# Attention and MLP layer on one core: order of the weights of the output product, of the MLP's first pair, of V's first lower halves and of the last product's additions

## The chip, the cores and the metric

The kernel runs on one core of a Trainium2 chip. A core has TensorE (PE in the profile; its weight loads are PEld), VectorE (DVE), ScalarE (ACT), GpSimd (POOL) and SyncE (SP), whose queue issues most of the DMAs; ScalarE issues some too. Each engine works through its own instructions in order and waits on semaphores for the others. TensorE writes into PSUM, eight banks of 128 x 512 f32; the other engines read it there. The metric is device time in microseconds, the median of several runs.

## The reference

One layer on x of 2048 tokens by 1024 features, in f32:

```
h  = x + attention(layernorm(x))       # 32 heads of 32, 4 segments of 512 tokens:
                                       # softmax inside the segment + a memory (M, z) carried over
                                       # segments, mixed by sigmoid(beta); then @ wo
h2 = h + gelu(layernorm(h) @ w1 + b1) @ w2 + b2      # w1 1024 x 3584, w2 3584 x 1024
```

## The kernel before

**Numbers in two halves.** Every matmul operand is kept as an upper half, rounded to fp32r by a cast, and a lower half, the rest, made by a subtraction. A product is three matmuls (upper x upper, upper x lower, lower x upper; `mm3`, `product`); such a group of three over 128 x 512 is the smallest step below. The cast is ScalarE's or VectorE's, the subtraction VectorE's or GpSimd's (`split`, lines 91 to 96).

**Stages.** A loop goes over two halves of 1024 tokens. In each: attention for 8 groups of 4 heads and two segments; the output product for the first segment (`wo_first`), woven into the last heads; the output product for the second segment (`wo_second`), woven into the first segment's second layer norm; the MLP's first product. After both halves comes the MLP's second product for all tokens (`Second`). Both MLP products save multiplications by forming sums of blocks and seven products instead of eight (Strassen-Winograd). So operands are sums of weight blocks or of token blocks, made by GpSimd or VectorE before they are split.

**What sets the order.** In attention and in `wo_second` a scheduler of the framework orders each engine's instructions at compile time, by their place in the program and by when it estimates their data to be ready; TensorE's order in `wo_second` is pinned to the program's (`in_order`, line 99). From the MLP's first product on, every engine's order is the program's. Python generators weave two streams: `interleave(main, side, ratio)` advances the side stream by `ratio` steps per step of the main one.

**Start of the second half.** `weights(0)` (line 630) loads the first group's blocks of wk, wq and wv (512 KB each, two raw buffers, tag wr), casts the uppers and has GpSimd make each lower half in one piece (line 96). `dense` multiplies them by the first segment's normalised tokens: keys (kps), queries (qps), values (vps), eight groups each. Woven in at 1.1 side steps per group is `ln1(half, 1)`, the second segment's layer norm: for each of four tiles of 128 tokens bn_stats on VectorE, mean and variance to scale and offset in three small GpSimd operations (`ln_scale`, `ln_offset`, lines 133 to 139), an activation (line 168), then two times four transposes on TensorE, a cast (149) and a subtraction (151). The keys of the second segment follow and need all four tiles.

**`wo_second`** computes eight blocks (n, t), n the half of the output columns and t the tile of tokens, in the order (0,0) (0,1) (1,0) (1,1) (0,2) (1,2) (0,3) (1,3), eight groups each. The weights come as four pieces k per n, 512 KB each, through the same two raw buffers. The pieces of n = 1 are called for in groups 1 and 5 of the blocks (0,0) and (0,1). A hook loads the MLP's first raw weights (`begin`, line 901) into the same buffers, a later one casts and subtracts them (909, 915).

**MLP, first product.** `lead` (line 927) goes through 14 steps. A step loads w1's block j + 3, casts block j + 2, does four groups of its upper part (c1) and subtracts its lower half (915), then four groups of c2 and the gelu (882), whose result goes to DRAM from ScalarE's queue. The last two steps have no c1. Woven in at 0.4 steps per group is `ln2_last`: the second segment's layer norm, transposed, and its combinations T1 to T4 (lines 814 to 838), some eleven VectorE operations for each of four tiles. When it is done, `fetch(0)` loads the raw blocks of the first of 14 pairs and a partial product saved before (p1). A table `todo` hangs three things on steps:

```
todo = {11: lambda: mixer.combine(0), 12: lambda: mixer.fetch(1),
        13: lambda: (mixer.made(0, "S2", "S1", "S3", "A22", "S4"), mixer.combine(1))}
```

`combine` makes four sums on GpSimd (980 to 983), `made` splits five blocks (cast 995, subtraction 996). Each `pair(j)` then has four-group products on PSUM banks bps and dps; u (1010) and u3 (1022) copy the bps bank out while the product goes on accumulating in it, so the next product of that bank waits for them.

**MLP, second product.** `Second` runs 112 jobs of 21 matmuls: two passes over the hidden features, each with seven products of eight token pairs. The products "1" and "7" of a pair, and "6" and "5", share a bank: the later one adds into it after the earlier one's result has been added to the output. In the loop (line 1261) come, for job n, `product(n)` on TensorE, then `work(n)`: loads, `sums` (GpSimd, 1165 to 1174), `prep(n + 2)`, which casts and subtracts the left operand of the job after next (1188, 1189), `fill_up(n)`, which makes right operands from w2 rows (GpSimd 1117, cast 1119, subtraction 1120), further loads; then `add(n)`, which adds the job's bank to output tiles c on VectorE (1257). The tiles c are loaded from DRAM up to two jobs ahead (1202). During the last pair, `prep(0)` and `prep(1)` are done after its groups 8 and 11.

Of the kernel before, what the change touches and what calls it, by code (L numbers as in the profile page):

```python
# [42 lines left out]
def build(tc, x, wq, wk, wv, wo, beta, w1, b1, w2, b2, out):  # L43
# [300 lines left out]
    def attention(half, first):  # L344
# [285 lines left out]
        def weights(g):  # L630
            ws = {}
            for n, w in (("k", wk), ("q", wq), ("v", wv)):
                ws[n] = load_block(wp, w, g * P, 3, "vector" if g or n == "k" else "scalar")
            return ws

        ws = first or weights(0)
        prev = None
        for g in range(NG):
            for sl in range(2):
                u = {"g": g, "s": 2 * half + sl}  # L640
                d = dense(g, sl, ws, u)
                if prev is None:
                    interleave(d, ln1(half, 1, aside=ws.pop("rest", None)), 1.6 if first else 1.1)
                    if first:
                        constants()
                    if "last" in acts:
                        acts.pop("last")
                else:
                    if g == NG - 1 and sl == 1:
                        d = hooked(d, lambda k: load_o(half, 0, k, ab), 3, NG - 1)  # L650
                    interleave(d, heads(prev), 1.0)
                prev = u
            if g + 1 < NG:
                ws = weights(g + 1)
# [29 lines left out]

    def wo_raw(n, k):
        wr = wp.tile([P, DC, P], F32, tag="wr", name="wr", bufs=2).rearrange("p a b -> p (a b)").rearrange("p (c n) -> p c n", c=2)
        nc.sync.dma_start(wr, wo[k * 256:(k + 1) * 256, n * 512:(n + 1) * 512].rearrange("(c p) n -> p c n", p=P))
# [58 lines left out]

    def wo_second(half, hts, ready):

# [283 lines left out]
    class Second:  # L1032
# [243 lines left out]
    for half in range(2):  # L1276
# [35 lines left out]

        second = wo_second(half, hts1, ready)
        load_x(half, 1, hts1)
# [6 lines left out]
        def ln2_last():  # L1321
# [3 lines left out]
            for n, _ in enumerate(side):  # L1325
# [6 lines left out]
        side, acc = ln2_last(), 0.0  # L1332
        todo = {11: lambda: mixer.combine(0), 12: lambda: mixer.fetch(1),
                13: lambda: (mixer.made(0, "S2", "S1", "S3", "A22", "S4"), mixer.combine(1))}
        for _ in mixer.lead():
            acc += 0.4
            while side and acc >= 1.0:
                acc -= 1.0
                if next(side, 0) == 0:
                    side = None  # L1340
                    pp.release()
                    mp = mixer.mp = tc.alloc_tile_pool(name=f"m1{half}", bufs=1, side="right", reuse_waits="tile")
                    mixer.fetch(0)
            if mixer.step in todo and not side:
# [12 lines left out]
        else:  # L1357
# [3 lines left out]
            for j in range(HP):  # L1361
# [3 lines left out]
                for n, _ in enumerate(mixer.pair(j)):  # L1365
# [44 lines left out]
```

## Time and profile before

| | us |
|---|---|
| median of 3 runs | 2328.36 |
| lowest and highest | 2328.06, 2329.9 |
| the profiled execution's own time | 2327.21 |
| its span, first to last instruction | 2325.4 |
| TensorE busy in the span | 2279.2 |

The profile is of one execution; its times are from the span's start. Stages in it: attention of the first half to about 550, `wo_second` to about 620, MLP lead to 703, pairs to 900; the second half's to 1435, 1505, 1588 and 1782; then the last product. A row of a timeline has start, duration, engine, line, operation, output <- inputs, shapes, and in brackets the engine's idle time before it and what ended that. A row of a table of waits has who waited for whom, the total, the times and the longest. "Granted clock" is the share of full speed at which TensorE was clocked.

### The profile page before, as it was taken

Reading aid. Unit: us, or ns where it says so; the run is one execution under the profiler, and the core shown is the slowest. Engines: PE = TensorE matmul, PEld = TensorE weight load, DVE = VectorE, ACT = ScalarE, POOL = GpSimd, SP = SyncE. Lnnn points to the kernel's source line nnn. Section 1 sums busy time; section 2 is a strip of 40 time slices with the busy share of each in tenths; the row PEclk is TensorE's granted clock in tenths of the full one; section 3 lists DMA queues with packets and bytes.
Section 4 is the critical chain, followed back from the end, with each engine's and each line's share of the span. In section 5 each row is a group of like instructions: output and inputs, shape, how many; then the busy total and the mean of one; then the engine's idle time right before and its main releaser. Section 6 shows DMA issues by size and latency. Waiting matters only on the chain.

```text
span 2325.4 us, 35324 instructions
## 1 busy us (share of the span) xinstructions
PE 2279.2 (98%) x11769; PEld 1891.8 (81%) x11769; DVE 1566.8 (67%) x3295; ACT 1232.5 (53%) x2561; POOL 1021.0 (44%) x1053
## 2 busy tenths in 40 slices
PE   8999999999999999999999999999999999999999
PEld 6888888878778887888888877778887888888887
DVE  7777777776655565777777777564566776567653
ACT  6777777775453445777777776363343223323321
POOL 5444555554104442555555556203444554156440
PEclk9999999999999999999999999999999999999999
DMA  6333333345365655333333344466667976577762
GB/s 192 87 85 88 91 91 84 83 131 184 116 207 168 187 162 146 105 90 85 84 90 85 84 110 149 141 199 176 172 182 265 332 253 201 167 245 238 245 220 93
DMA packets 322721, 355.36 MB, mean 153 GB/s; under 512 B 26191, under 2 KB 218731, under 8 KB 322539
## 3 DMA queue, kind: packets, MB, share of 16 engines
q1 hardware_dynamic: 259370, 316.40, 45.2%
q10 hardware_dynamic: 63168, 36.71, 5.3%
q8 instruction: 93, 1.52, 0.3%
q14 instruction: 90, 0.73, 0.1%
HBM read 226.59 MB, written 76.09 MB: 130 GB/s over the span
## 4 chain that ended last, share of the span: by engine, by line
PE 75%; DVE 9%; ACT 7%; issue 3%; DMA 3%; POOL 2%; SPq 0%; ACTq 0%; POOLq 0%; DVEq 0%
PE po L1247 22%; PE bps L865 8%; PE dps L865 5%; PE ppt L564 5%; PE po L584 5%; PE cps L865 3%; PE vps L120 2%; PE vps L119 2%; PE vps L121 2%; PE pqk L532 2%; PE kps L119 2%; PE kps L121 2%; PE kps L120 2%; ACT pr L541 2%; DVE ptl L571 2%
## 5 line engine op out<-in xcount | busy, mean ns | idle before, releaser
L548 POOL TENSOR_SCALAR pr<-pr,nm,gate 128x128 f32<-128x128 f32 (+3 forms) x512 | 320.2, 635 | 360.5 <-DVE nm L545 272.2
L541 ACT ACTIVATE pr<-pr,mx 128x256 f32<-128x256 f32 (+3 forms) x512 | 287.7, 562 | 164.4 <-DVE mx L533 161.4
L571 DVE TENSOR_TENSOR ptl<-ppt,pth 128x512 fp32r<-128x512 f32 (+1 forms) x384 | 228.0, 600 | 81.8 <-ACT pth L566 77.3
L533 DVE CUSTOM_DVE_ANT_0 pr<-pqk,mask 128x256 f32<-128x256 f32 (+3 forms) x512 | 243.6, 484 | 39.7 <-PE pqk L532 37.9
L564 PE MATMUL ppt<-ident,pr 128*128 128x128 f32 x1280 | 222.7, 277 | 1.5 <-DVE ptl L571 1.1
L566 ACT CAST pth<-ppt 128x512 fp32r<-128x512 f32 (+1 forms) x384 | 193.6, 516 | 37.3 <-PE ppt L564 30.7
L1257 DVE TENSOR_TENSOR c<-c,po 128x512 f32<-128x512 f32 x160 | 105.3, 683 | 150.6 <-PE po L1247 150.6
L564 PEld LDWEIGHTS ppt<-ident,pr 128*128 128x128 f32 x1280 | 164.0, 140 | 32.2 <-DVE ptl L571 2.1
L96 POOL TENSOR_TENSOR wl<-wr,wh 128x1024 fp32r<-128x1024 f32 x53 | 126.8, 2392 | 85.9 <-DVE wh L93 33.6
L532 PE MATMUL pqk<-ks,qs 96*128 96x256 f32 (+3 forms) x512 | 161.4, 316 | 0.2 <-DVE mx L533 0.2
L584 PE MATMUL po<-ptl,vs 128*64 128x512 f32 (+3 forms) x512 | 154.1, 311 | 5.1 <-DVE ptl L571 4.4
L584 PE MATMUL po<-pth,vs 128*64 128x512 f32 (+3 forms) x512 | 155.9, 327 | 1.2 <-ACT pth L566 1.1
L980 POOL TENSOR_TENSOR s<-r 128x512 f32<-128x512 f32 x28 | 42.9, 1532 | 233.0 <-DVE sa L996 77.2
L1247 PE MATMUL po<-w2h,zh 128*128 128x512 f32 x378 | 120.7, 389 | 0.0
L1117 POOL TENSOR_TENSOR w2r<-w2r 128x512 f32<-128x512 f32 x54 | 87.5, 1633 | 61.7 <-DMA w2r<-in_B_w 53.9
L532 PEld LDWEIGHTS pqk<-ks,qs 96*128 96x128 f32 x512 | 96.2, 188 | 21.6 <-DVE mx L533 0.7
L865 PE MATMUL bps<-zh,sa 128*128 128x512 f32 x336 | 110.8, 391 | 1.9 <-DVE u L1010 1.9
L865 PE MATMUL bps<-zh,sb 128*128 128x512 f32 x336 | 111.0, 391 | 0.9 <-DVE u L1022 0.9
L119 PE MATMUL vps<-yh,wh 128*128 128x512 f32 x256 | 109.4, 427 | 1.1 <-DVE MZ L499 1.1
L119 PE MATMUL kps<-yh,wh 128*128 128x512 f32 (+1 forms) x264 | 110.0, 417 | 0.0
L119 PE MATMUL qps<-yh,wh 128*128 128x512 f32 x256 | 107.1, 418 | 0.0
L1247 PE MATMUL po<-w2h,hl 128*128 128x512 f32 x322 | 102.9, 389 | 1.5 <-DVE c L1257 1.5
(239 smaller groups left out, 6626.5 us busy)
## 6 DMA issues: line engine op xcount, KB each, us to landing
hr<-h_dram SPq DMA_DIRECT2D x112, 448.0 KB, 4.8
w2r<-in_B_w SPq DMA_DIRECT2D x122, 256.0 KB, 4.4
r<-in_B_w SPq DMA_DIRECT2D x56, 512.0 KB, 4.6
h_dram<-ht ACTq DMA_DIRECT2D x84, 256.0 KB, 3.8
ks<-kh SPq DMA_DIRECT2D x256, 64.0 KB, 2.0
qs<-qh SPq DMA_DIRECT2D x256, 64.0 KB, 2.0
wr<-in_A_wo SPq DMA_DIRECT2D x32, 512.0 KB, 4.0
wx<-in_B_w SPq DMA_DIRECT2D x56, 256.0 KB, 4.0
```

Source lines behind the costliest of these rows:

```text
L96: getattr(nc, lo_eng).tensor_tensor(lo, w, raw(hi), op=ALU.subtract)
L119: nc.tensor.matmul(ps, ah, bh, start=first, stop=False)
L532: nc.tensor.matmul(pqk[:, :n], u["qs"][j][:, i * P:(i + 1) * P], u["ks"][j][:, 0:n], start=True, stop=True)
L533: nc.vector.tensor_tensor_reduce(out=st["pr"][:, offs[i]:offs[i] + n], in0=pqk[:, :n], in1=mask[:, 512 - n:512], op0=ALU.add, op1=ALU.min, ...
L541: nc.scalar.activation(pi, pi, AF.Exp, bias=mx[:, i:i + 1], scale=-1.0, accum_out=mx[:, 4 + i:5 + i])
L548: nc.gpsimd.tensor_scalar(pi, pi, nm[:, 4 + k:5 + k], gate[:, 1, 4 * g + j:4 * g + j + 1], op0=ALU.mult, op1=ALU.mult)
L564: nc.tensor.transpose(ppt[:, o:o + P], pr[:, offs[i] + jk * P:offs[i] + (jk + 1) * P], ident)
L566: nc.scalar.copy(pth[:, base:base + w], ppt[:, :w])
L571: nc.vector.tensor_tensor(o, x0, x1, op=ALU.subtract)
L584: nc.tensor.matmul(po[:, P * jk:], v, st[part][:, koff[jk]:koff[jk] + w], start=(jk, part) == (0, "pth"), stop=(jk, part) == (2, "ptl"))
L865: nc.tensor.matmul(ps, x_[:, c, :], y_[:, c, :], start=first and c == 0 and n == 0, stop=last and c == 3 and n == 2, skip_group_check=True)
L1247: nc.tensor.matmul(ps, x_[:, k], y_[k], start=opens and k == 0 and i == 0, stop=closes and k == self.KP - 1 and i == 2, skip_group_check=True)
```

## The change

1. Start of the second half: the value block's lower half is no longer made in `weights(0)`. It is made in two pieces of four chunks on GpSimd, hung behind the scale and offset of the layer norm's tiles 1 and 2 (`rest`). `ln1` there yields eight times between its loads and its first statistics, and goes at 1.5 side steps per group, not 1.1. (The first half's start, with its own `first`, is as before.)
2. `wo_second`: all four pieces of n = 1 are called for in block (0,0), in groups 1, 3, 5 and 7; pieces 0 and 1 land in two raw buffers of the pool `post`, pieces 2 and 3 in the old ones.
3. MLP lead: `ln2_last` goes at 0.3 steps per group; `fetch(0)` and `combine(0)` come in step 9, `made(0)` and `fetch(1)` in step 12, `combine(1)` in step 13.
4. `Second`: `prep(2)` is done after group 12 of the last pair, and no longer in job 0. `add(n)` comes after the loads, `sums` and `prep(n + 2)`, ahead of `fill_up(n)` and what follows it, which are now `after`. The stores and spills kept for later are taken up before `work`, as before.

```
-            for n, w in (("k", wk), ("q", wq), ("v", wv)):
+            for n, w in (("k", wk), ("q", wq)) + ((("v", wv),) if g else ()):
                 ws[n] = load_block(wp, w, g * P, 3, "vector" if g or n == "k" else "scalar")
+            if g == 0:
+                wr, wh, wl = [wp.tile([P, DC, P], t, tag=n, name=n, bufs=b) for n, t, b in (("wr", F32, 2), ("wh", F32R, 3), ("wl", F32R, 3))]
+                nc.sync.dma_start(wr, wv[:, 0:P].rearrange("(c p) n -> p c n", p=P))
+                nc.scalar.copy(wh, wr)
+                ws["v"] = wh, wl
+
+                def rest(t):
+                    if 0 < t < 3:
+                        k = slice(4 * t - 4, 4 * t)
+                        op = nc.gpsimd.tensor_tensor(wl[:, k], wr[:, k], raw(wh)[:, k], op=ALU.subtract)
+                        tc.add_manual_dep(op.ins, acts["nb"].ins.name, NOSYNC, reason="program order")
+
+                ws["rest"] = rest
...
-                    interleave(d, ln1(half, 1, aside=ws.pop("rest", None)), 1.6 if first else 1.1)
+                    interleave(d, ln1(half, 1, 8 * half, aside=ws.pop("rest", None)), 1.6 if first else 1.5)
...
-            wr = acts["raw"][k] if n == 0 and k < 2 else wo_raw(n, k)
+            wr = acts["raw"][k] if n == 0 and k < 2 else wo_raw(n, k, pp if n and k < 2 else wp)
...
-                    if n == 0 and t < 2 and g % 4 == 1:
-                        weights(1, 2 * t + g // 4)
+                    if n == 0 and t == 0 and g % 2 == 1:
+                        weights(1, g // 2)
...
         def work(self, n):
-            late, self.later = self.later, []
             self.rows_ahead(n)
             self.load_items(n)
             self.sums(n, n + 2)
-            self.prep(n + 2)
+            if n:
+                self.prep(n + 2)
+
+        def after(self, n, late):
             self.fill_up(n)
...
                 got = self.product(n)
+                late, self.later = self.later, []
                 self.work(n)
                 self.add(*got)
+                self.after(n, late)
...
-        todo = {11: lambda: mixer.combine(0), 12: lambda: mixer.fetch(1),
-                13: lambda: (mixer.made(0, "S2", "S1", "S3", "A22", "S4"), mixer.combine(1))}
+        todo = {9: lambda: (mixer.fetch(0), mixer.combine(0)), 12: lambda: (mixer.made(0, "S2", "S1", "S3", "A22", "S4"), mixer.fetch(1)),
+                13: lambda: mixer.combine(1)}
         for _ in mixer.lead():
-            acc += 0.4
+            acc += 0.3
...
-                    mixer.fetch(0)
...
-                    if (j, n) in ((HP - 1, 8), (HP - 1, 11)):
-                        second.prep(n // 10)
+                    if (j, n) in ((HP - 1, 8), (HP - 1, 11), (HP - 1, 12)):
+                        second.prep(n // 10 + n // 12)
```

More of the change, by code (lines that the diff above doesn't have):

```diff
@@ L683, in load_x, with wo_raw @@
             nc.sync.dma_start(hts[t], x[0, r0:r0 + P, :])
-    def wo_raw(n, k):
-        wr = wp.tile([P, DC, P], F32, tag="wr", name="wr", bufs=2).rearrange("p a b -> p (a b)").rearrange("p (c n) -> p c n", c=2)
+    def wo_raw(n, k, pool=None):
+        wr = (pool or wp).tile([P, DC, P], F32, tag="wr", name="wr", bufs=2).rearrange("p a b -> p (a b)").rearrange("p (c n) -> p c n", c=2)
         nc.sync.dma_start(wr, wo[k * 256:(k + 1) * 256, n * 512:(n + 1) * 512].rearrange("(c p) n -> p c n", p=P))
@@ L745, in wo_first, with wo_second @@
             pass
-    def wo_second(half, hts, ready):
+    def wo_second(half, hts, ready, pp):
         wts, blk = {}, {}
@@ L1311, in ready @@
                 last_token.append(steps)
-        second = wo_second(half, hts1, ready)
+        second = wo_second(half, hts1, ready, pp)
         load_x(half, 1, hts1)
```

## The prediction

> **What bounds the kernel now.** I read the page first, then the table of what TensorE waited for, then the busy time of chosen stretches.
>
> ```profile
> span 2325.4 us, 35324 instructions
> PE 2279.2 (98%) x11769; PEld 1891.8 (81%) x11769; DVE 1566.8 (67%) x3295; ACT 1232.5 (53%) x2561; POOL 1021.0 (44%) x1053
> ```
>
> TensorE is busy for 98% of the span, so an edit that removes no matmul can win only from the 46.2 us in which it sits idle (2325.4 - 2279.2) and from clock lost after idle. This change removes no matmul. The next table says which work ended the idle time; columns are total, times, longest.
>
> ```profile
> PE po L1247 <- DVE c L1257: 4.8, 2, 3.3
> PE cps L865 <- DVE wl L915: 4.6, 4, 2.0
> PE pwo L119 <- DVE zl L151: 3.6, 4, 1.6
> PE bps L865 <- DVE u L1010: 1.9, 2, 1.1
> PE pt L147 <- ACT xt L168: 1.9, 1, 1.9
> PE pwo L120 <- POOL wl L96: 0.9, 2, 0.6
> ```
>
> Each row is touched by one edit. The stretches place them (columns: length, then busy time of PE, PEld, DVE, ACT, POOL, granted clock, DMA share, GB/s).
>
> ```profile
> 626.00:666.00 40.00, 37.98 (x179) 30.51 (x179) 34.76 (x50) 27.85 (x43) 0.54 (x2) 1.00 0.57 172
> 666.00:703.00 37.00, 37.00 (x165) 30.62 (x164) 8.11 (x8) 16.80 (x25) 5.08 (x4) 1.00 0.85 256
> 900.00:925.00 25.00, 23.13 (x114) 19.08 (x113) 14.69 (x28) 16.82 (x24) 10.41 (x20) 0.93 0.58 164
> 1511.00:1551.00 40.00, 37.43 (x177) 30.14 (x176) 34.78 (x50) 27.99 (x43) 0.13 (x1) 1.00 0.53 164
> 1775.00:1800.00 25.00, 20.87 (x85) 16.84 (x85) 14.12 (x16) 7.82 (x10) 12.65 (x7) 0.93 1.00 339
> 1850.00:1875.00 25.00, 23.47 (x104) 19.14 (x103) 21.51 (x18) 6.79 (x10) 16.96 (x9) 1.00 0.74 254
> ```
>
> In two of them the granted clock is 0.93, and 0.07 x 25 us = 1.75 us is lost beside the idle time. **At stake** in all: 4.5 (3.6 + 0.9, output product) + 4.6 (cps) + 1.9 (first pair) + 3.65 (1.9 + 1.75, layer norm) + 6.55 (4.8 + 1.75, last product) = 21.2 us. No edit can give more than its share of this.
>
> **Output product's weights sooner (both halves, 4.5 us).** No work is added; four loads of 512 KB, casts and subtractions are issued within one block instead of two, on SP ahead of the stores of h + b2 that stood between them, and two of the loads land in buffers of their own.
>
> ```profile
> 575.39 2.65 SPq L687 DMA_DIRECT2D wr<-in_A_wo  x2
> 582.27 5.90 SPq L901 DMA_DIRECT2D wx<-in_B_w  x4
> 585.87 1.35 DVE L915 TENSOR_TENSOR wl<-wx,wh 128x512 fp32r<-128x512 f32 x1 [3.03 <-ACT wh L909]
> 588.93 1.27 DVE L151 TENSOR_TENSOR zl<-pt,zh 128x512 fp32r<-128x512 f32 x2
> ```
>
> The last two of the four loads are issued at 575.4 and about 577.7, because all four share two buffers; only when the third has been split can the MLP's first load go (582.27), and VectorE stands idle 3.03 us for it in front of L915. The layer norm's zl at 588.93, which frees the PSUM bank TensorE waits for, is queued behind. With two buffers more each buffer serves one turn less, and the issue is one block of 24 matmuls, about 5 us, sooner; that covers the 3.03 us. Late next is VectorE itself, whose three statistics (L126) still stand ahead of zl. Gain 3.0, two thirds, since the order on these engines is a scheduler's and four casts in one block crowd ScalarE. Bounds: 4.5, and -1.0 (the wait for wl doubled by the crowd).
>
> **Side work's pace in the MLP's first product, 0.4 to 0.3 (4.6 us).** In 626 to 666 VectorE is busy 34.76 of 40 us, in 666 to 703 only 8.11 of 37, and TensorE loses 40 - 37.98 = 2.02 us in the first, 40 - 37.43 = 2.57 in the other half.
>
> ```profile
> L915 DVE TENSOR_TENSOR wl<-wx,wh 128x1024 fp32r<-128x1024 f32 x6 | 7.3, 1219 | 0.0
> ```
>
> Of the 34.76 us, 7.3 are the weights' own lower halves; the other 27.4 are the layer norm's combinations. At 0.3 they spread over 4/3 of the time: 27.4 x 3/4 + 7.3 = 27.9 of 40, 70% instead of 87%. The cover is the slack after 666. Gain 4.0, bounds 4.6 and 2.0 (half the waits come from bursts inside a tile, which stay); no loss, as nothing is added and the weights' share comes no later.
>
> **First pair (1.9 us).** The pair's loads go from the side work's end to step 9, its sums from step 11 to 9, its halves from step 13 to 12; a step here is 5.4 us, the last two 2.7.
>
> ```profile
> 668.68 1.29 POOL L980 TENSOR_TENSOR s<-r 128x512 f32<-128x512 f32 x1 [42.04 <-ACT ht L882]
> 697.94 0.69 ACT L882 ACTIVATE ht<-cps,b1c 128x512 f32<-128x512 f32 x1 [2.13 <-PE cps L865]
> 702.45 3.00 DVE L996 TENSOR_TENSOR sa<-s,sa 128x512 fp32r<-128x512 f32 x3 [7.41 <-ACT sa L995]
> 705.38 1.77 DVE L996 TENSOR_TENSOR sa<-r,sa 128x512 fp32r<-128x512 f32 x1
> 703.28 1.62 POOL L980 TENSOR_TENSOR s<-r 128x512 f32<-128x512 f32 x1 [29.44 <-DVE sa L996]
> 708.78 0.68 DVE L1010 TENSOR_TENSOR u<-bps,p1r 128x512 f32<-128x512 f32 x1
> ```
>
> The five halves run from 702.45 beside GpSimd's sums of the second pair, and u (708.78), which TensorE waits for, stands behind them; the fourth takes 1.77 us. Elsewhere the same operation takes 0.69 (the fill at 1788.52, quoted below). One step sooner they start behind the activation of 697.94, at about 699, and five end by 702.5, before GpSimd starts at 703.28. The risk is the loads, three that go on SP behind a weight load of their step: step 9 is about 703 - 2 x 2.7 - 3 x 5.4 = 681; landing near 689 and four sums of 1.29 give 694, still 5 us ahead. Gain 1.6, bounds 0 and 1.9.
>
> **Second half's V lower halves behind layer norm (3.65 us).** GpSimd does two halves of 512 columns, 2 x 1.29, instead of one 2.40: 0.2 us more, off the path.
>
> ```profile
> 901.19 2.40 POOL L96 TENSOR_TENSOR wl<-wr,wh 128x1024 fp32r<-128x1024 f32 x1 [0.33 <-ACT wh L95]
> 903.68 0.19 POOL L133 TENSOR_SCALAR v<-mv 128x1 f32<-128x1 f32 x1
> 904.91 2.51 ACT L168 ACTIVATE xt<-xt,nb,v 128x1024 f32<-128x1024 f32 x2 [3.17 <-POOL nb L139]
> 902.46 0.19 DVE L130 BATCH_NORM_AGGREGATE mv<-st 128x2 f32<-128x12 f32 x1
> ```
>
> ```profile
> 904.90:923.10 18.20, 16.90 (x85) 14.27 (x86) 9.85 (x19) 14.56 (x21) 5.52 (x15) 0.91 0.56 159
> 1800.00:2275.00 475.00, 473.47 (x2089) 391.58 (x2088) 308.25 (x329) 139.13 (x184) 218.57 (x109) 1.00 0.71 237
> ```
>
> The statistics are ready at 902.65; v waits until 903.68 for V's lower half, so the activation could start 1.0 us sooner. A matmul takes 475 / 2089 = 0.227 us, a group of three 0.68. The delay of 8 side steps at 1.5 a group puts the first transpose in the program at group 13 / 1.5 = 9 instead of 5 / 1.1 = 5, 2.7 us later, which takes the rest of the 1.9 us wait. But ScalarE caps the gain. From the activation to the next product of keys, which needs all four tiles (923.1), it is busy 14.56 of 18.20 us; TensorE without its 1.3 us of idle time and 0.09 x 18.2 = 1.6 of clock would be there in 15.3. Of 3.65 I take 2.0: 1.0 from the start, 1.0 from ScalarE's 3.6 us of slack. V's raw buffer comes free some 5 us later (two tiles on), and so does SP for what stands behind the next block's load into it. Bounds 3.65, and -1.5 if this or the later start costs about half of ScalarE's slack.
>
> The Trainium skill (TensorE: Matmul & The Clock Gate, Part 1, the "warmup" mystery) lets the clock drop after an idle window of about 3.4 us; here 1.9 us of idle time were enough for 0.93 over 25 us, so the measurement decides. By the page this edit would have 1.9 us at stake, and the sum would be 0.1 us less.
>
> **Third left operand in the last pair, additions first (6.55 us).** On VectorE alone the order changes: operand, addition, fill instead of operand, fill, addition; GpSimd, ScalarE and SP keep theirs, but for one operand (a cast, a subtraction) that moves ahead of the last pair's end.
>
> ```profile
> 1787.87 0.62 ACT L1119 CAST zh<-w2r 128x512 fp32r<-128x512 f32 x1 [0.45 <-ACT ht L882]
> 1783.88 2.17 DVE L1189 TENSOR_TENSOR zh<-hr,zh 128x896 fp32r<-128x896 f32 x1
> 1788.52 0.69 DVE L1120 TENSOR_TENSOR zl<-w2r,zh 128x512 fp32r<-128x512 f32 x1 [1.86 <-ACT zh L1119]
> 1789.13 0.68 DVE L889 TENSOR_TENSOR ht<-dps,u 128x512 f32<-128x512 f32 x1
> 1791.98 1.09 DVE L1189 TENSOR_TENSOR zl<-hr,zl 128x896 fp32r<-128x896 f32 x1 [2.17 <-ACT zl L1188]
> 1792.99 1.28 DVE L1257 TENSOR_TENSOR c<-c,po 128x512 f32<-128x512 f32 x2
> ```
>
> The third job adds into the bank that the first addition (1792.99) reads; TensorE resumes at its end, 1794.4. In the changed order the operand's cast takes the fill's place on ScalarE at 1787.87 and lasts 1.1 us (0.62 x 896/512); its subtraction (1.09) ends at 1790.1, the fill (0.69) and L889 (0.68) at 1791.4, the two additions (1.28) at 1792.7. TensorE starts 1.6 us sooner and still waits 1.7. Waits of up to 2.0 us left the clock at 1.00 in 1511 to 1551, so of the 1.75 us I take 1.2 as saved. The second wait, 4.8 - 3.3 = 1.5 us in 1850 to 1875, ends with an addition that the program puts behind fills, and goes: 1.3. Gain 4.1, bounds 6.55 and 0: the DMA share here is 1.00, and the operand frees its buffer a job sooner, so that a load goes on SP ahead of rows to be added, which may come as late as the additions do now.
>
> **Sum.** 3.0 + 4.0 + 1.6 + 2.0 + 4.1 = 14.7 us. The profiled execution took 2327.21 us, so 2312.5; the median of the runs, 2328.36, lies 1.15 above it, so **2313.7 us**.
>
> **Rivals.** (1) DMA takes over around 1775 to 1850, and the last product's 4.1 us stay as waits for loads: 2317.8. For it, the share of 1.00; against it, that VectorE's row names an addition, not a load. (2) The second half's opening is held by ScalarE, and gives -1.5 instead of 2.0: 2317.2. (3) The scheduler puts the weights and the side work where they were: their 3.0 + 4.0 stay: 2320.7. Against it, the MLP part's order is written out. (4) **Slower**: additions first leave VectorE idle in front of each addition with fills ready behind it, and these then run beside GpSimd's sums of the next operand.
>
> ```profile
> L1257 DVE TENSOR_TENSOR c<-c,po 128x512 f32<-128x512 f32 x146 | 95.9, 682 | 120.9 <-PE po L1247 120.9
> L1120 DVE TENSOR_TENSOR w2l<-w2r,w2h 128x512 fp32r<-128x512 f32 x56 | 63.4, 1144 | 15.8 <-ACT w2h L1119 15.4
> L1189 DVE TENSOR_TENSOR zh<-hr,zh 128x896 fp32r<-128x896 f32 x33 | 46.0, 1394 | 11.5 <-ACT zh L1188 11.2 <-DMA w2r<-in_B_w 0.3
> ```
>
> These 475 us hold about 100 jobs of 21 matmuls, 4.77 us each. A job now has 1.46 additions of 0.68, one operand of about 1.3 and 0.84 fills of 1.1: 3.2. Were every operand (2.17) and fill (1.77) to meet GpSimd, a job with two additions would have 1.36 + 2.17 + 1.77 = 5.3, 0.5 above TensorE's; where half the jobs are such, 25 us are lost, and 2328.4 - 10.6 + 25 = 2343. It decides from 10.6 / 0.5 = 21 such jobs on. The 308.25 us of 475 that VectorE works today speak against it. The Trainium skill (SBUF, section "SBUF: two separate sides") has VectorE's operations on two SBUF inputs and GpSimd's shut each other out for whole instructions, which speaks for (4); 0.69 against 1.77 agrees, and by the page every such meeting costs all of the other's length, up to 1.3 us.
>
> **Chances.** Forecast 0.60, (1) 0.14, (2) 0.11, (3) 0.10, (4) 0.05. A measurement of this kernel can tell about 0.2%, 4.7 us, from no change. The range goes from all 21.2 us won, 2307, to 2323, where (1) and (3) come together for the most part (4.1 + 7.0 missing: 2324.8). Faster than 2323.7: nearly all of the forecast, most of (1) to (3): 0.84; same 0.11; slower 0.05.
>
> **What would show it.** Right: no wait of cps for wl, of pwo for zl, of bps for u L1010 in TensorE's table; clock 1.00 at both openings; about 1.7 us left before the third job. Wrong: the waits return under DMA names or as kps behind yh in the second half; L1120 much above 1.1 us; TensorE's idle time still above 35 us.

## The result and the profile after

The changed kernel takes 2312.46 us (median of 6 runs, 2311.59 to 2315.3) against 2328.21 us for the kernel before on the same chip (6 runs, 2326.47 to 2332.54): a ratio of 0.993, 95% interval 0.992 to 0.994. Forecast were 2313.7 us, with 2307 to 2323 as the range. The profiled execution of the changed kernel has a span of 2309.8 us, 15.6 us less than before.

The head of its page:

```profile
span 2309.8 us, 35321 instructions
PE 2276.1 (99%) x11769; PEld 1890.8 (82%) x11769; DVE 1560.3 (68%) x3295; ACT 1232.0 (53%) x2561; POOL 1025.9 (44%) x1054
```

TensorE's idle time is 33.7 us (2309.8 - 2276.1) where it was 46.2. The rows of the table of TensorE's waits that answer to the six of before (who waited for whom, total, times, longest):

```profile
PE po L1262 <- DVE c L1272: 1.8, 1, 1.8
PE pwo L119 <- DVE zl L151: 1.0, 3, 0.5
PE bps L878 <- DVE u L1035: 0.9, 1, 0.9
PE pt L147 <- DVE yl L151: 0.9, 1, 0.9
PE pt L147 <- ACT xt L168: 0.2, 1, 0.2
```

Gone are cps for wl, pwo for the POOL wl, and bps for the first pair's u. The wait before the third job of the last product is 1.8 us instead of 3.3. The layer norm's 1.9 us is gone, and a new wait of 0.9 us (the row of yl, at 908.1) stands in the second half's opening; the 0.2 us for xt lies at 25.7, in the first half, where the kernel before waits 0.15. The row of bps for L1035 is in the last pair and was there before. The stretches that answer to those of before:

```profile
626.00:666.00 40.00, 40.00 (x191) 33.07 (x190) 33.10 (x47) 27.26 (x43) 0.00 (x0) 1.00 0.55 173
1495.00:1535.00 40.00, 40.00 (x193) 33.09 (x193) 30.65 (x44) 25.28 (x38) 1.80 (x3) 1.00 0.56 173
880.00:925.00 45.00, 44.02 (x220) 35.86 (x219) 23.77 (x55) 25.95 (x46) 19.11 (x27) 1.00 0.53 144
1776.53:1779.95 3.42, 1.61 (x8) 1.04 (x7) 2.44 (x6) 1.70 (x3) 0.00 (x0) 1.00 0.92 311
1779.95:1783.36 3.41, 3.41 (x10) 2.67 (x9) 3.28 (x4) 0.81 (x1) 0.00 (x0) 0.50 0.60 167
```

TensorE no longer pauses in the first 40 us of the MLP; the clock stays at 1.00 in the second half's opening; but behind the wait for the third job it still runs at 0.50 for 3.41 us (such a stretch is called a dip below).

**Where the 15.6 us came from.** I take the start of the same matmul in each trace as a boundary between stages (the last of attention, the first into cps, into bps, of the second half's kps, the vps product that waits 1.1 us for MZ, the first of the last product's L1262), and subtract. The changed kernel was profiled a second time (further down as the repeat).

| stage, us | before | after | repeat | gain, first and repeat |
|---|---|---|---|---|
| `wo_second`, both halves | 69.42 + 69.75 | 67.30 + 68.10 | 67.78 + 68.30 | 3.8, 3.1 |
| MLP lead, both | 82.81 + 83.32 | 80.01 + 80.01 | 80.03 + 80.01 | 6.1, 6.1 |
| pairs, both | 189.95 + 193.30 | 188.85 + 191.89 | 188.85 + 191.89 | 2.5, 2.5 |
| second half's opening | 50.74 | 47.98 | 47.98 | 2.8, 2.8 |
| last product | 543.93 | 542.20 | 541.05 | 1.7, 2.9 |
| attention, both (not edited) | 550.95 + 491.24 | 551.44 + 492.03 | 552.20 + 491.17 | -1.3, -1.2 |
| sum | | | | 15.6, 16.2 |

Lead, pairs and opening come out the same to some 0.1 us in every execution that shares their code. The other stages do not: over all the runs below the first attention takes 550.7 to 552.5 us, the two `wo_second` together 135.4 to 137.0 where their code is the changed kernel's, and the last product 540.4 to 544.4 in the seven executions of the changed kernel's code for it. So a whole span says little about an edit worth 2 us, and the experiments are read by stages.

### The profile page after: what moved, and what is told of

The parts are those of the page before. It is cut to its first block, busy times and chain, and to the rows that moved or that the text cites. A ratio compares the mean times of both kernels' runs of the same rounds, so it can differ in the third digit from the quotient of the medians.

```text
span 2309.8 us, 35321 instructions
## 1 busy us (share of the span) xinstructions
PE 2276.1 (99%) x11769; PEld 1890.8 (82%) x11769; DVE 1560.3 (68%) x3295; ACT 1232.0 (53%) x2561; POOL 1025.9 (44%) x1054
## 4 chain that ended last, share of the span: by engine, by line
PE 76%; DVE 7%; ACT 7%; DMA 4%; issue 3%; POOL 3%; SPq 1%; ACTq 0%; POOLq 0%; DVEq 0%
PE po L1262 20%; PE bps L878 8%; PE cps L878 7%; PE dps L878 6%; PE ppt L564 5%; PE po L584 5%; PE vps L120 2%; PE vps L119 2%; PE vps L121 2%; PE pqk L532 2%; PE kps L119 2%; PE kps L120 2%; PE kps L121 2%; ACT pr L541 2%; DVE ptl L571 2%
## 5 line engine op out<-in xcount | busy, mean ns | idle before, releaser
L1262 PE MATMUL po<-w2h,zh 128*128 128x512 f32 x378 | 121.0, 390 | 0.0
L1262 PE MATMUL po<-w2h,hl 128*128 128x512 f32 x322 | 103.0, 389 | 0.2 <-DVE hl L1202 0.2
```

Of the source, the lines that this page charges most:

```text
L1262: nc.tensor.matmul(ps, x_[:, k], y_[k], start=opens and k == 0 and i == 0, stop=closes and k == self.KP - 1 and i == 2, skip_group_check=True)
```

## The experiments

Times in the table are medians with the ratio to the kernel before, timed beside each. Their intervals all overlap, so none of these edits is told from the changed kernel by time alone.

| run | median | ratio, 95% interval | span |
|---|---|---|---|
| layer norm as before | 2313.68 | 0.9938, 0.9923 to 0.9953 | 2311.0 |
| weights as before | 2313.29 | 0.9935, 0.9920 to 0.9949 | 2310.1 |
| pace 0.4 | 2316.88 | 0.9944, 0.9927 to 0.9960 | 2315.4 |
| first pair as before | 2314.14 | 0.9940, 0.9925 to 0.9955 | 2316.9 |
| fills first | 2315.28 | 0.9951, 0.9936 to 0.9966 | 2312.5 |
| operand late | 2315.62 | 0.9948, 0.9933 to 0.9963 | 2309.4 |
| V's halves only | 2311.17 | 0.9934, 0.9917 to 0.9951 | 2308.6 |
| last fill later | 2309.85 | 0.9931, 0.9916 to 0.9946 | 2307.1 |
| two fills later | 2313.24 | 0.9930, 0.9917 to 0.9943 | 2312.4 |
| the repeat | 2313.47 | 0.9932, 0.9918 to 0.9945 | 2309.2 |
| operand sooner | 2310.52 | 0.9925, 0.9910 to 0.9939 | 2310.1 |

**Layer norm as before.**

```
-interleave(d, ln1(half, 1, 8 * half, aside=...), 1.6 if first else 1.5)
+interleave(d, ln1(half, 1, aside=...), 1.6 if first else 1.1)     # and V's lower half in one piece again
```

> The changed kernel, with the second half's start as it was: V's lower half in one GpSimd piece ahead of the layer norm, no delay, 1.1 side steps a group. Nothing computed changes. Theory (the five parts add up, each worth what its own wait and its own clock dip cost): the wait of pt for xt in the layer norm is back at about 1.9 us, pt for yl (0.9) goes, and TensorE's records in 880 to 925 show the clock below 1.00 again; span about 2.6 us longer than the 2309.8 us of the changed kernel, so 2312.4. Rival (the parts share a slack, so that what one gives another would have given): less than 1 us longer. Rival on the clock (a dip depends on where a gap falls, not on its length alone): the wait is back but the clock stays at 1.00, and the span is only about 1 us longer.

The wait, and the stretch of 880 to 925 in this run:

```profile
PE pt L147 <- ACT xt L168: 1.9, 1, 1.9
```

```profile
880.00:925.00 45.00, 43.03 (x205) 35.30 (x203) 22.18 (x49) 24.51 (x40) 15.60 (x24) 0.96 0.54 155
```

Wait and dip are back, and the opening takes 50.79 us, 2.8 more than with the edit. The span is only 1.2 us longer, because the third job's wait happened to be 1.07 us here, with no dip behind it. The theory holds for the stage.

**V's halves only.** The two pieces stay behind the layer norm's small operations, with the delay and the pace of before.

```
-interleave(d, ln1(half, 1, 8 * half, aside=...), 1.6 if first else 1.5)
+interleave(d, ln1(half, 1, aside=...), 1.6 if first else 1.1)
```

> The changed kernel, with V's lower halves still behind the layer norm's small operations on GpSimd, but the layer norm's own delay and pace at the second half's start as before (none, 1.1 side steps a group). Nothing computed changes. Theory (the two edits share the gain: v comes 1.0 us sooner by GpSimd's order, the rest by putting the first transpose later in TensorE's program): pt for xt is about 0.9 us, the clock stays at 1.00 and the span is about 0.7 us longer than 2309.8. Rival A (GpSimd's order alone did it): no wait and the same span. Rival B (the delay alone did it): pt for xt at 1.9 us as before, and about 2.6 us longer.

```profile
PE pt L147 <- ACT xt L168: 1.1, 2, 0.9
```

The opening takes 48.96 us. So GpSimd's order alone gave 1.8 of the 2.8 us (50.74 - 48.96), the delay and pace the other 1.0. The wait of 1.87 us fell to 0.9, as v came about 1 us sooner, and that took the dip with it.

**Weights as before.**

```
-wr = ... else wo_raw(n, k, pp if n and k < 2 else wp)
+wr = ... else wo_raw(n, k)
-if n == 0 and t == 0 and g % 2 == 1: weights(1, g // 2)
+if n == 0 and t < 2 and g % 4 == 1: weights(1, 2 * t + g // 4)
```

> The changed kernel, with the output product's second weights called for as before: two pieces in each of the blocks (0,0) and (0,1), all through the two old raw buffers. Nothing computed changes. Theory (parts add up): the waits pwo for zl (3.6 us in all) and pwo for wl (0.9) are back in place of the 1.0 that is left; span 3.5 us longer than 2309.8, so 2313.3. Rival (the slower pace of the side work in the MLP's first product already gives the room, and this part gives little): under 1.5 us longer.

```profile
PE pwo L119 <- DVE zl L151: 3.4, 4, 1.5
```

The waits for zl are back (3.4 us, against 1.0 in the first profile and 1.4 in the repeat), those for the POOL wl (0.9) are not. The two stages take 68.72 + 69.06 = 137.8 us, 2.4 more than in the first profile of the change and 1.7 more than in the repeat, but 1.4 less than before. So this edit is worth about 2 us, between the theory's 3.5 and the rival's 1.5, and some 1.4 of that stage's gain seems to have come with the other edits. These are single executions of a stage that moves by up to 1.6 us with its code unchanged, so neither size is sharp. The order there is a scheduler's, which sees the whole program; what exactly it moved stays open.

**Pace 0.4.**

```
-acc += 0.3
+acc += 0.4
```

> The changed kernel, with the side work of the MLP's first product at 0.4 steps per group again. Nothing computed changes. Theory (VectorE at 87% of 40 us there makes its bursts late for the weights' lower halves): cps for wl is back with about 4 waits and 4.6 us, VectorE is busy 34 to 35 of the 40 us after the output product, and the span is 4.6 us longer than 2309.8, so 2314.4. Rival (the waits came from the late weights of the output product, which pushed the layer norm and the first lower halves back; with those sooner the old pace costs little): under 2 us longer.

```profile
PE cps L878 <- DVE wl L928: 3.8, 4, 1.4
```

```profile
627.00:667.00 40.00, 38.18 (x178) 30.68 (x178) 35.27 (x51) 27.84 (x43) 0.00 (x0) 1.00 0.49 151
1507.00:1547.00 40.00, 38.07 (x178) 30.58 (x176) 35.15 (x51) 28.06 (x44) 0.00 (x0) 1.00 0.49 150
```

VectorE is back at 35.27 of 40 us. The leads take 82.58 + 82.72 us, 5.3 more than at 0.3. That is more than the waits: they are 3.8 us. A wait's idle time counts from the modelled end of the matmul before. At the changed kernel's third job:

```profile
1776.68 0.39 PE L1262 MATMUL po<-w2l,zh 128*128 128x512 f32 x1
1776.91 0.39 PE L1262 MATMUL po<-w2h,zh 128*128 128x512 f32 x1
1779.11 0.47 PE L1262 MATMUL po<-zh,zl 128*128 128x512 f32 x1 [1.81 <-DVE c L1272]
```

Matmuls start every 0.23 us and are shown as 0.39 long. The start that should have come at 1777.14 came at 1779.11: 1.97 us lost, 1.81 shown. Each wait hides 0.16 us in this way, and one shorter than 0.16 us isn't shown at all. In the leads the matmul behind the one that waited is late as well: at pace 0.4 one that waited started at 646.25 and the next at 646.59, 0.34 us later and not 0.23. So a wait there costs 0.27 us more than its row says, and two more, of 0.03 and 0.04 us (at 658.28 and 1538.53), cost 0.15 each and have no row: 3.8 + 4 x 0.27 + 2 x 0.15 = 5.2 of the 5.3 us.

**First pair as before.** The table `todo` of before, and `fetch(0)` at the side work's end.

> The changed kernel, with the MLP's first pair called for as before: its loads at the end of the side work, its sums in step 11, its halves in step 13; the pace stays at 0.3. Nothing computed changes. Theory (parts add up): bps for u is back with 2 waits; at 0.3 the side work ends later than at 0.4, and the loads with it, so 1.9 us at the least and up to 4; span 2311.7 to 2314. Rival (the slower pace alone takes VectorE's other work out of the halves' way): under 1 us longer.

```profile
PE bps L878 <- DVE u L1023: 1.6, 2, 0.8
PE bps L878 <- DVE u L1035: 0.9, 1, 0.9
```

The pairs take 189.93 + 193.01 us, 2.2 more; the theory's 1.9 to 4 holds and the rival falls. The span is 7.1 us longer, but nearly all of the rest is in stages whose code was not touched: the last product took 544.37 us in this execution.

**Fills first.**

```
 def after(self, n, late, got):
     self.fill_up(n)
     ...
     self.ahead(n)
+    self.add(*got)           # no longer ahead of after
```

> The changed kernel, with each job's additions behind its fills again; the third left operand stays in the last pair. Nothing computed changes. Theory (order on VectorE sets both waits of the last product): the wait before the third job grows from 1.8 us by the fill that stands ahead of the additions, 0.7 to 1.3 us, the second wait of 1.5 us near 1860 is back, and the clock dips at the third job as before; span 2 to 3 us longer than 2309.8, so about 2312.3. Rival (additions first does nothing after the first jobs, since VectorE has slack there): 0.7 to 1.3 us longer, with one wait.

```profile
PE po L1263 <- DVE c L1273: 5.4, 2, 3.9
```

```profile
1851.21 1.27 DVE L1273 TENSOR_TENSOR c<-c,po 128x512 f32<-128x512 f32 x2
1852.40 1.08 DVE L1202 TENSOR_TENSOR hl<-hr,hl 128x896 fp32r<-128x896 f32 x1
1853.41 5.08 DVE L1133 TENSOR_TENSOR w2l<-w2r,w2h 128x512 fp32r<-128x512 f32 x2
1858.41 0.68 DVE L1273 TENSOR_TENSOR c<-c,po 128x512 f32<-128x512 f32 x1
```

The cost is not where I put it. The third job waits 1.55 us, no more than with additions first, as no fill is due in the first jobs: the 14 that they need are made in the pairs. It is the second wait that comes back, at 3.9 us where it was 1.5 in the kernel before, and with a dip: two fills of 2.5 us each, slowed beside GpSimd, stand ahead of the addition of 1858.41 that TensorE waits for. The last product takes 544.8 us, 3.8 over the median of the seven executions (541.05).

**Operand late.**

```
-if n: self.prep(n + 2)
+self.prep(n + 2)             # and prep(2) no longer in the last pair
```

> The changed kernel, with the third left operand split in job 0 again; additions first stays. Nothing computed changes. Theory (the operand's subtraction stands ahead of the first addition wherever it is issued, and in the last pair it leaves the queue before the job's own operand): the wait before the third job grows from 1.8 to about 2.9 us, one operand of 1.1 us more on VectorE; span about 1.1 us longer than 2309.8, so 2310.9. Rival (the operand early gained nothing, because it is slowed beside GpSimd and pushes the last fill back): the same span within 0.3 us.

```profile
1773.49 0.69 DVE L1133 TENSOR_TENSOR zl<-w2r,zh 128x512 fp32r<-128x512 f32 x1 [1.86 <-ACT zh L1132]
1774.10 0.68 DVE L902 TENSOR_TENSOR ht<-dps,u 128x512 f32<-128x512 f32 x1
1776.95 1.09 DVE L1202 TENSOR_TENSOR zl<-hr,zl 128x896 fp32r<-128x896 f32 x1 [2.17 <-ACT zl L1201]
1777.96 1.28 DVE L1271 TENSOR_TENSOR c<-c,po 128x512 f32<-128x512 f32 x2
```

The operand (1776.95) is again the last thing ahead of the first addition, with 2.2 us of idle time in front of it. The wait is 2.24 us, and in this execution GpSimd's sums began early (5.39 us ahead of the last product), which in the repeat below goes with 0.74. Counted from that beginning the third job starts 17.3 us on (5.39 + 11.92), against 15.4 in the repeat; so the operand early is worth about 1.9 us there, more than the theory's 1.1. The gap of 2.24 us lowered no clock. The profiled execution, of 2311.1 us, is the fastest of four; the others took 2315.4 to 2316.3, and where they lost that no profile shows.

**Last fill later, two fills later.**

```
-(HP - 1, 1), (HP - 1, 5), (HP - 1, 9), (HP - 1, 13)]
+(HP - 1, 1), (HP - 1, 5), (HP - 1, 9)]          # last fill later
+(HP - 1, 1), (HP - 1, 8), (HP - 1, 9)]          # two fills later
```

> The changed kernel, without the last of the fills done during the last pair (after its group 13); it is then made in job 0, behind the additions. Nothing computed changes. In the changed kernel this fill's subtraction runs at 1768.59 to 1770.54, slowed beside GpSimd, ahead of the operand for the third job. Theory (VectorE's queue ahead of the first addition sets the wait, and a gap drops the clock only when it fills more than about half of a 3.41 us window of the clock's control): the wait before the third job shrinks from 1.8 to about 1.2 us and the clock stays at 1.00 there; span 2.3 us shorter than 2309.8, so 2307.5. Rival A (the clock drops after any gap here): 0.6 us shorter, clock still 0.72 around the gap. Rival B (the fill is needed soon and now comes late): no shorter, with a wait of po for a w2 half instead.

> The changed kernel, with the last of the fills done during the last pair left to job 0 (behind the additions), and the third-last one moved from behind group 5 to behind group 8, out of the way of the copy u that TensorE waited 0.9 us for. Nothing computed changes. Theory: the wait before the third job falls from 1.8 to about 0.7 us as with the first of these edits alone, so the clock cannot drop there in any execution; bps for u (0.9) goes too; span 0.9 us below that edit's 2307.1, so 2306.2, and the median 1.5 to 3 us below the changed kernel's of the same call. Rival (the fill in its new place delays the operands and moves the wait to another job): the same span as with one fill moved, or up to 1 us longer.

With one fill moved the third job waits 0.74 us (1.2 were expected) and the span is 2307.1, near the 2307.5 expected; but the repeat below shows 0.74 without the edit, so the wait alone does not show a gain. With two moved the span is 2312.4 where 2306.2 was expected, the waits are these (po for zh and hl are operands), and bps for L1035, which I wanted gone, stayed:

```profile
PE po L1262 <- DVE hl L1202: 1.7, 2, 1.5
PE po L1262 <- DVE zh L1202: 1.5, 2, 1.1
PE po L1262 <- DVE c L1272: 1.2, 1, 1.2
PE bps L878 <- DVE u L1035: 0.9, 1, 0.9
```

The rival holds: the longest wait for zh, 1.1 us, is in the second job, whose operand stands on VectorE behind two fills in a row (3.66 us). The last product takes 543.05 us, against 540.21 with one fill moved; the rest of the longer span is for the most part attention's.

**The repeat.**

> The changed kernel once more, nothing edited. In its first profile TensorE waits 1.81 us before the third job of the last product, and its clock shows 0.50 for the 3.41 us that follow. Theory (the clock is set for stretches of 3.41 us on a grid that has no fixed place against the kernel, by whether TensorE was idle for more than half of the stretch before): the same wait is there, and whether it lowers the clock is chance, about one execution in two; without it the span is 2308.2, with it 2309.8. Rival (the gap's length alone decides): the clock shows 0.50 after this wait again and the span is 2309.8 within 0.5 us.

The wait itself was not the same: 0.74 us in place of 1.81, and no dip. GpSimd's timeline in the first profile of the changed kernel, then in the repeat:

```profile
1763.68 2.12 POOL L1178 TENSOR_TENSOR hr<-hr 128x896 f32<-128x896 f32 x1 [13.29 <-DMA hr<-h_dram]
```

```profile
1763.24 2.13 POOL L1178 TENSOR_TENSOR hr<-hr 128x896 f32<-128x896 f32 x1 [13.57 <-DMA hr<-h_dram]
```

GpSimd has stood idle for 13 us until the raw token blocks land; from there its sums, the casts, VectorE's subtractions and the additions follow in one chain. Measured against the first matmul of the last product (1767.61 and 1768.19) it starts 3.93 us ahead in the one and 4.96 in the other. Over the seven executions whose code is the same there:

| GpSimd starts ahead of the last product by, us | 4.96 | 4.71 | 4.61 | 4.13 | 4.01 | 3.93 | 3.40 |
|---|---|---|---|---|---|---|---|
| third job waits, us | 0.74 | 0.98 | 1.07 | 1.90 | 1.69 | 1.81 | 1.75 |
| third job starts behind the last product's start, us | 10.42 | 10.66 | 10.75 | 11.58 | 11.39 | 11.50 | 11.96 |

The first and the last row add up to 15.36 to 15.43 us in six of the seven and to 15.71 in one: the third job starts 15.4 us after GpSimd does. So what is late behind this wait is a load, and when it lands differs by 1.5 us from execution to execution. (The wait itself is a poorer measure: with 3.40 ahead, 0.23 us of the lateness is already in a wait of the second job.) The same sum tells what an edit does to the chain, whenever the load lands. It is 17.3 us in the kernel before (4.37 + 12.94) and with the operand late, 15.4 with fills first (4.13 + 11.23), 14.8 with the last fill moved (4.34 + 10.42) and 16.5 with two moved (4.22 + 12.24). So at the third job the early operand is worth 1.9 us, additions first nothing, and the last fill 0.6, each from one execution.

**Operand sooner.** The last run tries to shorten that chain.

```
-if (j, n) in ((HP - 1, 8), (HP - 1, 11), (HP - 1, 12)):
-    second.prep(n // 10 + n // 12)
+if (j, n) in ((HP - 1, 8), (HP - 1, 11)):
+    for m in (0,) if n == 8 else (1, 2):
+        second.prep(m)            # and the last fill later, as above
```

> The changed kernel, with the third left operand split after group 11 of the last pair, right behind the second one, and not after group 12; and with the last of the fills left to job 0, behind the additions. Nothing computed changes. In the changed kernel VectorE stood idle for 2.2 us in front of this operand's subtraction (1775.48), because its cast stood behind a gelu on ScalarE that waits for VectorE's sum. Theory (the order on VectorE and ScalarE ahead of the first addition sets the wait before the third job; the landing of the raw rows that start GpSimd's sums sets how much it varies): the subtraction runs about 2 us sooner, the two additions end at about the end of the second job, the wait before the third job is 0 to 0.3 us instead of 0.7 to 1.9, and the clock has no gap to drop for; span 2306 to 2308, median 1 to 2.5 us below the changed kernel's. Rival A (GpSimd's sums beside it slow the subtraction to 2.2 us and hold the sum behind it by as much): wait about 0.7 us, as with the fill alone. Rival B (the moved work comes back as waits for operands or for halves of w2 in jobs 3 to 10): no wait before the third job, and the same span.

```profile
1771.60 2.96 POOL L1178 TENSOR_TENSOR hr<-hr 128x896 f32<-128x896 f32 x1
1772.50 3.00 DVE L1202 TENSOR_TENSOR zl<-hr,zl 128x896 fp32r<-128x896 f32 x1
```

Rival A. The subtraction runs 3 us sooner, but beside GpSimd's sum, and takes 3.00 us instead of 1.09. The wait is 0.65 us. GpSimd started 4.10 ahead and the third job 10.33 us into the last product, 14.4 us in all, so the two edits won about 1.0 us there, 0.6 of which the last fill gives alone; a wait of 2.1 us for an operand in a later job took them back. The median, 2310.52, and the ratio of 0.9925 cannot be told from the changed kernel's.

**Long gaps.** How long must TensorE be idle for its clock to drop? Extra work on VectorE made gaps of many lengths in the last product.

```
-nc.vector.tensor_tensor(l, src, raw(h), op=ALU.subtract)
+for _ in range(5 + n // 5 % 6 if n >= 20 and n % 5 == 0 else 1):
+    nc.vector.tensor_tensor(l, src, raw(h), op=ALU.subtract)
```

> The changed kernel, with VectorE's subtraction for the left operand repeated 5 to 10 times (the same values each time) in every fifth job of the last product from job 20 on. So TensorE waits some 18 times, for lengths between nothing and about 5 us, at places that have no fixed relation to the clock's stretches. Results do not change. Theory (a stretch of 3.41 us in which TensorE is idle for more than half lowers the clock for the next stretch): every wait of which more than 1.71 us falls within one stretch is followed by 3.41 us at 0.50; waits of 1.8 to 3.4 us that a boundary splits into parts below 1.71 us are not; none below 1.7 us is. Rival (a gap's own length, with some bound between 1.0 and 3.4 us): all gaps above one length are followed by a dip and none below it, wherever they fall. Rival 2 (the clock drops only after a whole idle stretch): only waits above 3.41 us show a dip.

Fewer gaps came out than meant, 12 of 1.2 to 13.7 us (one time of 2396.67 us, span 2394.9). In all traces the clock changes only at times that lie on one grid of 3.41 us within an execution, whose offset differs between executions. So I cut the stretches on that grid; the granted clock is the third number from the end:

```profile
1985.88:1989.29 3.41, 0.49 (x3) 0.30 (x3) 3.34 (x4) 1.20 (x2) 0.00 (x0) 1.00 0.01 2
1989.29:1992.71 3.42, 3.42 (x10) 2.64 (x9) 3.41 (x5) 0.00 (x0) 0.00 (x0) 0.50 0.81 261
...
2037.08:2040.49 3.41, 1.79 (x8) 1.14 (x7) 3.31 (x4) 0.94 (x1) 0.00 (x0) 1.00 0.00 0
2040.49:2043.91 3.42, 2.63 (x11) 2.17 (x12) 3.42 (x5) 0.00 (x0) 0.00 (x0) 1.00 0.11 37
2043.91:2047.32 3.41, 3.41 (x16) 2.82 (x15) 3.41 (x6) 0.62 (x1) 0.00 (x0) 1.00 0.84 246
2153.13:2156.55 3.42, 2.00 (x9) 1.31 (x7) 3.37 (x2) 1.79 (x3) 3.20 (x2) 1.00 0.00 0
2156.55:2159.96 3.41, 0.37 (x2) 0.32 (x3) 3.34 (x4) 0.71 (x2) 0.00 (x0) 1.00 0.00 0
2159.96:2163.37 3.41, 3.41 (x10) 2.64 (x9) 3.41 (x6) 0.00 (x0) 0.00 (x0) 0.50 0.80 199
```

A gap of 2.92 us within one stretch (1986.03 to 1988.95) was followed by 0.50. One of 2.40 us (2038.87 to 2041.28), split 1.62 and 0.78 by a boundary, was not: both stretches were busy for over half, and the clock stayed. One of 4.46 us, split 1.41 and 3.04, lowered the clock once. Since gaps of 1.81, 1.87 and 1.89 us inside one stretch did lower it in other traces (the first profile of the changed kernel, the kernel before, layer norm as before), length alone doesn't decide, and both rivals fall. The theory's half is near but not exact: a stretch with 1.72 us of idle time did not lower it (below).

## Why the prediction was right

The sum was 14.7 us and the spans gave 15.6 and 16.2, so the forecast holds; its terms were off by up to 2.4 us each, and that their sum came so near is in part luck: the first four stages gained 4.6 and 3.9 us more than was taken, while the last product gained 2.4 and 1.2 less and attention, which nobody edited and the sum put at nothing, took 1.3 and 1.2.

- **Output product's weights, 3.0 taken:** 3.8 and 3.1 in the stage, of which undoing the edit returns about 2. Right in size; but the claim that each row is touched by one edit was wrong, since the row of the POOL wl (0.9 us) stayed gone, and 1.4 us of the stage stayed won, without it.
- **Pace, 4.0 taken, 4.6 as the upper bound:** undoing it costs 5.3 us, and the leads gained 6.1. The mechanism is the one foretold (VectorE 35.27 of 40 us at 0.4, 33.10 and 30.65 at 0.3). The step that failed is "no edit can give more than its share of this": the sum at stake was made of idle time, which leaves out 0.27 us of each wait in the leads, and the shortest waits whole. The same holds for the **first pair**, 1.6 taken with a bound of 1.9: 2.5 in the stage, 2.2 by undoing.
- **Layer norm, 2.0 taken, bounds 3.65 and -1.5:** 2.8. GpSimd's order gave 1.8, the shorter wait and the dip that went with it together, where the text had 1.0. The delay gave 1.0, of which "the rest of the 1.9 us wait" is the size. Of the 3.65 us at stake 0.85 were not won, against the 1.65 allowed for, and what stands there now is the new wait of 0.9 us for yl, VectorE's, not ScalarE's; rival (2) falls.
- **Last product, 4.1 taken (1.6 + 1.2 + 1.3), bounds 6.55 and 0:** 1.7 in the first profile, 2.9 in the repeat. "TensorE starts 1.6 us sooner and still waits 1.7" was met by the first profile (1.8 left) and missed by 1.0 in the repeat, because the start of the chain is a load that lands when it lands; counted from there the 1.6 us are 1.9 (17.3 to 15.4), and the early operand gives them, as the text had it. The second wait, 1.3, is gone in both, and fills first, which brings it back at 3.9 us, shows that additions first is worth at least that. The mis-sized term is **the 1.2 us of clock**. Between the first and the eleventh job of the last product the first profile has 51.32 us (11.50 + 39.82) and the repeat 48.59; behind the third job's start, where neither has a wait of note, it is 39.82 against 38.17, so one dip cost 1.65 us. It was there in the first profile and absent in the repeat, and no single number was right for both. The reason given, that waits of up to 2.0 us left the clock alone in 1511 to 1551, was a true reading of a chance: the longest of them there, 1.98 us, had a boundary of the grid in its middle (1531.13), as these rows of the kernel before show:

```profile
1527.72:1531.13 3.41, 2.38 (x11) 1.63 (x9) 3.38 (x6) 2.51 (x5) 0.00 (x0) 1.00 0.21 77
1531.13:1534.54 3.41, 2.47 (x13) 2.05 (x14) 3.38 (x6) 2.15 (x4) 0.00 (x0) 1.00 0.62 171
1534.54:1537.95 3.41, 3.41 (x19) 2.80 (x18) 3.32 (x6) 2.32 (x4) 0.00 (x0) 1.00 0.44 141
```

- **Rivals.** (1) loads take over: not as waits of TensorE for loads, but it had the right place; what decides the third job's wait is a load. (3) the scheduler undoes it: no, the stage gained. (4) VectorE falls behind where operands and fills meet GpSimd: single ones do (5.08 us for two fills, 3.00 for an operand), yet with additions first the last product is 1.7 to 2.9 us shorter than before, not 25 longer. Of the signs named beforehand two were missed: pwo still waits 1.0 us for zl (1.4 in the repeat), and in the first profile the clock was not 1.00 at the last product's opening.

What stays open: which waits in attention move it by 1 to 2 us between executions, and why the last product took 544.4 us once. That execution's table has 5.2 us of po waits in it (1.9 for an addition, 3.3 for operands) where the repeat's has 2.6; what made those operands late is not shown.

## What to carry to other kernels

A wait's idle time in the table is a lower bound of what it costs; subtract the starts of the same instruction in two traces, stage by stage. Profile the same kernel twice before a term under 2 us is believed: here three stages repeated to 0.1 us and the others did not, and a load's landing was the reason in one; there it helped to count from the landing. When an order of work on VectorE was chosen here, the costly thing was not the number of operations ahead of the one that TensorE waits for but those among them that meet GpSimd (two fills of 2.5 us each, an operand of 3.00).

## What the runs showed of the clock

The granted clock is set for stretches of 3.41 us on a grid that runs on its own, with no fixed place against the kernel. Over the 14 traces, about 9,400 such stretches without each kernel's end, the clock of the next was 0.50 after every one in which TensorE was busy for less than 0.49 of the time (23 of them), and 1.00 after all others but two; the closest on either side are 0.485 (dropped) and 0.495 (kept). The two: one of 0.69 busy that dropped, at 1393 in the run with the first pair as before, and one of 0.70 in the long-gaps run, itself at half clock, that was followed by another at 0.50. At a kernel's end the rule broke once more: in the run with the first pair as before TensorE's last stretch, from 2311.5, was busy for 0.45, and the next was still at 1.00. These cases stay open. The closest pair of ordinary waits is the first profile of the changed kernel, 1.61 of 3.42 us busy around its gap of 1.81 us (dropped, quoted above), and V's halves only, with 1.69 us:

```profile
1775.77:1779.18 3.41, 1.72 (x8) 1.15 (x7) 2.86 (x5) 1.27 (x2) 0.00 (x0) 1.00 0.94 317
1779.18:1782.60 3.42, 3.42 (x17) 2.79 (x16) 3.00 (x4) 1.23 (x2) 0.00 (x0) 1.00 0.56 164
```

The wait of 1.81 us, which lost 1.97, therefore costs either 2.0 us or 3.6 (with the 1.65 of a dip), by chance. An estimate of that chance: some 1.74 us of it must fall in one stretch (the idle time of the two closest cases is 1.72 and 1.76), which 51% of its possible places give ((3.41 - 1.81) + 2 x (1.81 - 1.74) of 3.41). In the table's four executions with waits of 1.69 to 1.90 us the clock dropped in one. No lone gap below 1.72 us lowered the clock, the drop at 1393 apart, so cutting a wait from 1.9 to 1.6 us can be worth more than its 0.3. The Trainium skill (TensorE: Matmul & The Clock Gate, Part 1, the "warmup" mystery) has free-running windows of 3413 ns, and the grid agrees with that; it has the clock fall after at least one idle window, and here half of one was enough.
